# Weights' words and stores on ScalarE's queue, early words, unread products and a fifth weight buffer in an attention and Fourier-mixing kernel

## Chip, cores and metric

One core of one Trainium2 chip. The metric is the device time of one execution in microseconds (us). Each version was run several times; every run quoted here is fast (the program is on one core, and no run lay over 1.5% above the fastest of its kernel).

## The reference, cut to what matters

```python
B, H, S, Dh = 8, 8, 576, 64          # batches, heads, tokens, head width; D = 512
q_s = softmax(q, over Dh);  k_s = softmax(k, over S)
x   = q_s @ (k_s^T v)                # per batch and head, then heads side by side: (B, S, 512)
u   = x + real(fft2(x))              # over tokens and channels of a batch
un  = layer_norm(u)
out = u + relu(un @ w1) @ w2         # w1: 512 x 2048, w2: 2048 x 512
```

## The kernel before

The eight batches and one shared group of left-over tokens go through "rounds". A round has an **up phase** (un @ w1, relu) and a **down phase** (@ w2), each as seven half-size products (Strassen's scheme in Winograd's form). The attention, transform and normalising of the *next* batch are merged into these two phases as side steps. After the start TensorE has hardly a pause.

The weights arrive as 64-bit words. In the **start** they are converted once on the chip: 16 pairs of tiles (8 for w1, 8 for w2), each 2 halves of 128 x 512. A pair is converted, combined (four sums and differences) and stored to scratch memory (w1s, w2s), from which each round loads it again. What follows is cut.

```python
def wtile(self):                                   # ring of weight tiles, for words, pairs and reloads
    return self.work.tile([P, NP, HD], F32, tag="w", name="w", bufs=4)

def convert(self, place, t):                       # one half
    ...                                            # hi, lo: the two 32-bit halves of each word
    nc.scalar.activation(lo, lo.bitcast(U32), ACT.Copy, scale=2.0 ** -29)
    V.tensor_scalar(out=ti, in0=hi, ... shift left 3, and mask)
    V.scalar_tensor_tensor(out=ti, in0=hi, ... sign and top exponent bits | ti)
    nc.scalar.activation(hi, hi, ACT.Abs)
    V.scalar_tensor_tensor(out=t, in0=hi, scalar=least, in1=t, op0=is_ge, op1=mult)
    nc.gpsimd.tensor_tensor(out=ti, in0=ti, in1=lo, op=ALU.add)      # "the adder"

def prepare(self, layer, p, places):               # one pair
    w = self.wtile()
    for i in range(2): self.convert(places[i], ...)
    (b_side if layer else a_side)(..., nc.gpsimd, nc.vector)         # four combinations, split
    nc.sync.dma_start(w1s or w2s, w[:, 0:7, :])                      # SyncE issues the store

# per round g:
cut = len(side) * 2 // 3                           # two thirds of the next batch's steps in the up phase
merged(first (g == 0: with the weights) or up steps, side[:cut])
merged(down, side[cut:] + norm(g + 1))
```

## Time and profile before

| | before |
|---|---|
| median of 3 runs (range) | 1390.59 us (1386.94 to 1391.18) |
| span in the trace | 1384.5 us |
| first up-product / first down-product | 110.2 / 289.8 us |
| from the first down-product to the end | 1094.7 us |

The two times in the third row are the starts of the first matmul of the up line and of the down line in TensorE's timeline. They split the span into "start" and "rest". The lines of the profile are in the prediction.

### The profile page before, as it was taken

Reading aid. Unit: us, or ns where it says so; the run is one execution under the profiler, and the core shown is the slowest. Engines: PE = TensorE matmul, PEld = TensorE weight load, DVE = VectorE, ACT = ScalarE, POOL = GpSimd, SP = SyncE. Lnnn points to the kernel's source line nnn. Section 1 sums busy time; section 2 is a strip of 40 time slices with the busy share of each in tenths; the row PEclk is TensorE's granted clock in tenths of the full one; section 3 lists DMA queues with packets and bytes.
Section 4 is the critical chain, followed back from the end, with each engine's and each line's share of the span. In section 5 each row is a group of like instructions: output and inputs, shape, how many; then the busy total and the mean of one; then the engine's idle time right before and its main releaser. Section 6 shows DMA issues by size and latency. Waiting matters only on the chain.

```text
span 1384.5 us, 14661 instructions
## 1 busy us (share of the span) xinstructions
PE 1226.2 (89%) x5676; PEld 1003.1 (72%) x5676; DVE 580.0 (42%) x1146; ACT 326.7 (24%) x590; POOL 422.1 (30%) x350
## 2 busy tenths in 40 slices
PE   4578677399899998999999999999999999999992
PEld 3437563288787876788778877887788778788882
DVE  3948876821513254335713542364234242502200
ACT  2624342410310142114301421142014101201200
POOL 1624566710530125003600450045013401321310
PEclk7558785589999999999999999999999999999996
DMA  5922334575342543156424542454253335455421
GB/s 170 306 68 69 137 128 163 190 265 164 141 152 88 172 159 146 67 167 198 158 98 138 193 159 77 145 197 152 88 146 130 150 103 174 150 178 179 165 102 45
DMA packets 90279, 203.46 MB, mean 147 GB/s; under 512 B 22241, under 2 KB 56033, under 8 KB 82145
## 3 DMA queue, kind: packets, MB, share of 16 engines
q1 hardware_dynamic: 90208, 202.52, 43.2%
q8 instruction: 45, 0.74, 0.2%
q14 instruction: 26, 0.20, 0.0%
HBM read 177.33 MB, written 29.88 MB: 150 GB/s over the span
## 4 chain that ended last, share of the span: by engine, by line
PE 74%; DVE 10%; POOL 6%; DMA 4%; issue 2%; ACT 1%; SPq 0%; POOLq 0%; DVEq 0%; ACTq 0%
PE bb L590 14%; PE bb L555 11%; PE bc L590 9%; PE ba L590 9%; PE ba L555 7%; PE bc L555 6%; PE acc L402 5%; DMA q<-in_q_dram 3%; PE acc L289 3%; PE acc L427 2%; POOL w L192 1%; PE acc L424 1%; PE tr L486 1%; PE acc L405 1%; POOL eo L384 1%
## 5 line engine op out<-in xcount | busy, mean ns | idle before, releaser
L555 PE MATMUL bb<-unT,w 128*128 128x256 f32 x864 | 218.8, 395 | 46.6 <-DVE u L525 39.6
L555 PEld LDWEIGHTS bb<-unT,w 128*128 128x128 f32 x864 | 166.5, 197 | 78.3 <-DVE u L525 46.3
L590 PE MATMUL bb<-w,h 128*128 128x256 f32 x864 | 198.5, 381 | 0.0
L590 PEld LDWEIGHTS bb<-w,h 128*128 128x128 f32 x864 | 161.5, 190 | 28.4 <-issue 7.3
L555 PE MATMUL ba<-unT,w 128*128 128x256 f32 x576 | 142.5, 387 | 0.0
L196 POOL TENSOR_TENSOR h<-h 128x512 f32<-128x512 f32 x36 | 46.1, 1279 | 313.4 <-ACT h L567 313.4
L555 PE MATMUL bc<-unT,w 128*128 128x256 f32 x576 | 140.5, 381 | 0.0
L590 PE MATMUL bc<-w,h 128*128 128x256 f32 x576 | 131.4, 381 | 0.0
L590 PE MATMUL ba<-w,h 128*128 128x256 f32 x576 | 128.0, 379 | 0.0
L590 PEld LDWEIGHTS bc<-w,h 128*128 128x128 f32 x576 | 107.5, 190 | 18.0 <-issue 4.4
L555 PEld LDWEIGHTS ba<-unT,w 128*128 128x128 f32 x576 | 109.2, 194 | 15.7 <-issue 1.0
L590 PEld LDWEIGHTS ba<-w,h 128*128 128x128 f32 x576 | 109.2, 190 | 15.4 <-issue 0.8
L555 PEld LDWEIGHTS bc<-unT,w 128*128 128x128 f32 x576 | 107.0, 190 | 15.3 <-DVE h L566 0.9
L567 ACT ACTIVATE h<-h 128x512 f32<-128x512 f32 x108 | 68.1, 631 | 190.8 <-DVE h L566 190.5
L604 POOL TENSOR_TENSOR x<-x,u 128x512 f32<-128x512 f32 x18 | 23.3, 1293 | 254.4 <-DVE u L528 172.2
L402 PE MATMUL acc<-ft,eo 128*128 128x289 f32 (+3 forms) x240 | 83.3, 472 | 7.5 <-POOL eo L386 7.4
L402 PEld LDWEIGHTS acc<-ft,eo 128*128 128x128 f32 (+3 forms) x240 | 39.6, 183 | 42.3 <-issue 26.0
L525 DVE TENSOR_TENSOR u<-bb,s 128x512 f32<-128x512 f32 x45 | 31.0, 689 | 89.1 <-PE bb L555 54.3
L318 POOL TENSOR_TENSOR q<-q,qm 128x512 f32<-128x512 f32 x36 | 41.8, 1170 | 82.2 <-DVE qm L317 33.1
L528 DVE TENSOR_TENSOR u<-bb,s 128x512 f32<-128x512 f32 x45 | 31.0, 689 | 77.5 <-PE bb L555 45.4
L289 PE MATMUL acc<-v,ks 128*128 128x128 f32 (+1 forms) x320 | 55.5, 317 | 6.1 <-ACT ks L277 4.1
L566 DVE TENSOR_TENSOR h<-bc,u 128x512 f32<-128x512 f32 x72 | 49.6, 689 | 24.0 <-PE bc L555 23.0
(134 smaller groups left out, 1540.0 us busy)
## 6 DMA issues: line engine op xcount, KB each, us to landing
w<-w2s SPq DMA_DIRECT2D x63, 1024.0 KB
w<-w1s SPq DMA_DIRECT2D x64, 896.0 KB
k<-in_kT_dram SPq DMA_DIRECT2D x32, 288.0 KB
h<-in_w_dram SPq DMA_DIRECT2D x18, 512.0 KB
v<-in_v_dram SPq DMA_DIRECT2D x32, 256.0 KB
q<-in_q_dram SPq DMA_DIRECT2D x32, 256.0 KB
w1s<-w SPq DMA_DIRECT2D x8, 896.0 KB
w2s<-w SPq DMA_DIRECT2D x8, 896.0 KB
```

The source lines that it names most:

```text
L196: e1.tensor_tensor(out=at(4), in0=at(2), in1=at(3), op=ALU.add)
L289: nc.tensor.matmul(pk, lhsT=ks[0:n, c, :], rhs=v[0:n, c, :], start=(c == 0), stop=(c == NC - 1))
L318: nc.gpsimd.tensor_tensor(out=heads, in0=heads, in1=spread(m), op=ALU.subtract)
L402: nc.tensor.matmul(pz, lhsT=eo[c][int(odds)][s, cols], rhs=self.ft[s, 3 * int(odds) + c, :], start=(c == 0), stop=(c == 2 and odds))
L427: nc.tensor.matmul(pb, lhsT=z(2 + k), rhs=self.cd[:, 2 + k, 0:HD - 1], start=(k == 0), stop=(k == 1))
L525: V.tensor_tensor(out=temp("u2"), in0=box["bb"][:], in1=box["s1"][:], op=ALU.add)
L528: V.tensor_tensor(out=temp("u3"), in0=box["bb"][:], in1=box["s1"][:], op=ALU.add)
L555: nc.tensor.matmul(bank()[:, i, :], lhsT=w[:, A_AT[m], k * P:(k + 1) * P], rhs=unT[:, B_AT[m], k, :], start=first and i == 0 and k == 0, s ...
L566: V.tensor_tensor(out=at(i), in0=bank[:], in1=u[:], op=ALU.add)
L567: nc.scalar.activation(at(i), at(i), ACT.Relu)
L590: nc.tensor.matmul(bank()[:, i, :], lhsT=h[:, p, A_AT[m], i * P:(i + 1) * P], rhs=w[:, p, :], start=first and i == 0 and p == 0, stop=p == ...
L604: nc.gpsimd.tensor_tensor(out=x, in0=x, in1=t[:], op=ALU.add)
```

## The change

Its intent: shorten the start, in which TensorE idles, by preparing the weights earlier and with less work on GpSimd. ScalarE's queue issues the words' loads and the stores of combinations, so that they don't stand among SyncE's loads; words of seven pairs are fetched during the first attention; the conversion loses one two-input instruction; all combinations go to VectorE; the first batch's queries have six buffers in place of three; 30 unread products keep the array busy; and only one third of the second batch's steps is merged into the first up phase. Smaller parts are that a tail's first query rows come in one transfer, and that each pair's store is issued one pair later. One line deepens the ring of weight tiles from four to five.

```diff
-        return self.work.tile([P, NP, HD], F32, tag="w", name="w", bufs=4)
+        return self.work.tile([P, NP, HD], F32, tag="w", name="w", bufs=5)
 ... words():  self.nc.sync.dma_start  ->  self.nc.scalar.dma_start
 ... convert(place, t, adder):
+        nc.scalar.activation(t, hi.bitcast(F32), ACT.Abs)
+        V.tensor_scalar_max(t, t, least)
+        V.tensor_scalar(out=ti, in0=ti, ... shift left 3, and mask)
         V.scalar_tensor_tensor(out=ti, in0=hi, ... | ti)
+        nc.scalar.activation(lo, lo.bitcast(U32), ACT.Copy, scale=2.0 ** -29)
+        adder.tensor_tensor(out=ti, in0=ti, in1=lo, op=ALU.add)          # adder: GpSimd, as before
-        (...)(lambda i: w[:, i, :], nc.gpsimd, nc.vector)
+        (...)(lambda i: w[:, i, :], self.nc.vector, self.nc.vector)
+    def send(self, layer, p, w):                   # called one pair later
+        self.nc.scalar.dma_start(to, w[:, 0:7, :])
+    def warm(self, t, n):                          # n unread products of 128 x 128 x 256
+    def follow(self, t):                           # after a key's or query's exponential:
+        if self.first:                             # touch the place (gate), then fetch early words
+            self.nc.scalar.copy(place[0:1, 0:1], t[0:1, 0:1]); run()
-        q = self.work.tile([P, D], F32, tag="q", name="q", bufs=3)
+        q = self.halves()[:, 0:D]                  # first batch: ring of six
-        cut = len(side) * 2 // 3
+        cut = len(side) * (1 if g == 0 else 2) // 3
```

## The prediction

> **What bounds the kernel now.** I read the engine totals first, then busy time by stretch, then waits and groups inside the first stretch, then the queue that issues the transfers. The totals say TensorE, but an average over stages can hide a stage with another limit. So I cut the span where the programme changes: attention of the first batch (to 62 us), its transform and normalising (to 110), the first batch's up-products (to 204), the rest of the weights' preparation (to 290), and everything after.
>
> ```profile
> PE 1226.2 (89%) x5676; PEld 1003.1 (72%) x5676; DVE 580.0 (42%) x1146; ACT 326.7 (24%) x590; POOL 422.1 (30%) x350
> ...
> PEclk7558785589999999999999999999999999999996
> ```
>
> ```profile
> core 0: us, PE busy (x) PEld busy (x) DVE busy (x) ACT busy (x) POOL busy (x), PEclk, DMA share, GB/s
> 0.00:62.00 62.00, 27.33 (x114) 21.32 (x115) 37.81 (x79) 24.44 (x44) 22.76 (x30) 0.66 0.75 240
> 62.00:110.00 48.00, 34.59 (x91) 18.86 (x90) 28.31 (x65) 16.47 (x31) 16.25 (x15) 0.57 0.31 100
> 110.00:204.00 94.00, 70.14 (x341) 59.99 (x340) 77.31 (x126) 34.23 (x63) 52.27 (x43) 0.86 0.32 108
> 204.00:290.00 86.00, 52.81 (x161) 33.83 (x160) 59.30 (x113) 29.97 (x53) 50.61 (x42) 0.54 0.62 204
> 290.00:1384.50 1094.50, 1041.38 (x4977) 869.05 (x4975) 377.24 (x765) 221.60 (x401) 280.21 (x221) 0.98 0.42 143
> ```
>
> The last row is 95% TensorE at a granted clock of 0.98: the change can win almost nothing there. The first 290 us hold 185 us of TensorE, partly at half clock. There VectorE is busiest (203 us of 290, 77 of 94 while the first up-products run). Everything to be won is in these 290 us. The waits there say why TensorE stands:
>
> ```profile
> PE tr L486 <- DVE eo L479: 34.0, 3, 23.3
> PE bb L555 <- DVE u L525: 23.9, 3, 8.7
> ```
>
> The first are transposes waiting for normalised rows, the longest (23.3 us) while VectorE works off weights. The second are up-products whose PSUM bank VectorE empties late because weights stand ahead of it in its queue. The weights' own groups:
>
> ```profile
> L192 POOL TENSOR_TENSOR w<-w,h 128x512 int32<-128x512 int32 x18 | 25.9, 1444 | 26.9 <-DVE w L191 23.7 <-DVE qrec L322 2.5 <-issue 0.7
> L191 DVE SCALAR_TENSOR_TENSOR w<-h,w 128x512 f32<-128x512 f32 x18 | 22.1, 1232 | 1.2 <-ACT h L190 1.1
> L187 DVE SCALAR_TENSOR_TENSOR w<-h,w 128x512 int32<-128x512 int32 x18 | 16.4, 914 | 0.0
> ```
>
> VectorE is almost never idle before its two (1.2 and 0.0 us), and both run above their undisturbed 0.69 us (seen at 83.6 and 85.1 us, where GpSimd is still). The end of the stage is one chain: the last combination is stored, lands, is loaded again, and only then may the down-products start:
>
> ```profile
> 275.77 0.38 SPq L219 DMA_DIRECT2D w2s<-w  x1
> ...
> 280.52 2.12 SPq L230 DMA_DIRECT2D w<-w2s  x4
> ```
>
> The first down-product starts at 289.8 us: 14 us after that store was issued.
>
> **What the Trainium skill says.** "SBUF — State Buffer", section "Who interferes with whom": a VectorE instruction with two SBUF inputs, or in a 2-port mode, excludes a GpSimd instruction that reads SBUF, and one blocks the other wholly. The trace agrees: L191 has a mean of 1.23 us against 0.69 undisturbed. "VectorE: DVE Perf Modes", section "Mode 2×_2P": one-source fp32 instructions get two elements a cycle, two-source ones don't. The trace agrees: a one-source instruction on 512 columns (L185) takes 0.42 us, a two-source one 0.69. "DMA: Bandwidth & Descriptors", section "Issuing engines are not separate DMA queues": issuing from another engine saves only the sequencer's time. I take from this that ScalarE issuing brings no bandwidth, but frees transfers from the waits of SyncE's queue. "TensorE: Matmul & The Clock Gate", section "HAM oscillation": idle gaps over some 3.4 us return the array to half clock. The trace agrees in direction: after a 3.5 us gap at 68.5 us the transform's products run at about 0.57 us each, against 0.28 at 206 us.
>
> **The change, part by part.**
> (1) Conversion: per half tile of 128x512, 0.42 + 0.69 + 0.69 = 1.80 us on VectorE become 0.42 + 0.42 + 0.69 = 1.53, as a maximum with a constant replaces a two-source comparison. 32 halves save 8.6 us.
> (2) Combinations: all four per pair go to VectorE. Before, GpSimd had two of four in layer 1 and three of four in layer 2. Undisturbed, 256 columns cost VectorE 0.40 us: 8 x 2 + 8 x 3 = 40 instructions add 16 us to VectorE and take 40 x 0.87 = 35 us from GpSimd (L196, L197, L203, L205 and L206 have means of 0.82 to 0.89). So VectorE's own demand grows by 16 - 8.6 = 7.4 us. In return the alternation VectorE, GpSimd, VectorE, GpSimd per pair is gone, and less GpSimd work blocks VectorE: in the start VectorE was busy 203 us for some 172 us of undisturbed durations, so blocking was about 30 us; GpSimd's 142 us there fall by 35, a quarter, so about 8 us of it go. The two sums cancel. The gain must come from order.
> (3) Order. The changed kernel's instruction order, as built, shows the first words' loads at the head of ScalarE's queue (before: issued at 25.4 us), stores no longer between SyncE's loads (SyncE waited 62.9 us for them at L216 and 42.4 at L219), and the second batch's queries, fold, transform and normalising behind the last weights on VectorE, most of the products of these inside the first down-products on TensorE. That takes from the start about 35 us of VectorE work (queries 4 x 2.4, folds and copies 6, mix 5, normalising and combining 9, keys of the third batch 6).
> (4) The unread products. The description announces 36; the build has 30 (four key tiles, two tail and four query tiles, three each), or 60 in the trace. At 0.43 us warm, 0.86 cold, that is 13 to 26 us beside attention's waits; TensorE is busy 27 of the first 62 us. If they keep the array warm through the transform, its 18 + 10 products take about 13 us instead of 28.
>
> Now the new start, from summed durations along VectorE's order. To the first combining of the normalised tile it holds 74 us (before 64, reached at 112 us). Attention itself no longer waits for query tiles (a six-deep ring instead of three) or for ten small loads: I put its end at 50 us instead of 62, and the start of the up-products at 98 instead of 110, VectorE-bound, since stalls and blocking fill the 24 us above the sum. Up-products: 48 us of TensorE (224 products of 0.216 x 2), 8 us of keys of which I count 4 as hidden in stalls, and bank waits: after the first and third group VectorE converts two pairs (2 x 4.7 us plus keys) ahead of the emptying of the next, while TensorE can go on for 5.2 us (12 products): 6 + 8 us. That makes 66 us, to 164 (before: 94). Two of layer 2's pairs are then done. The other six: two buffers, each bound for a load of about 6.5 us (1 MB) and 6 us of conversion, so 6.3 us a pair where it was about 11 (stores issued at 226.5, 237.2, 248.1): 164 + 5 for the first load + 38 = 207. Then the 14 us of store and load, tied with the last queries, which need about as long: the down-products start at 221 instead of 290, **69 us earlier**.
>
> Given back: TensorE work that was done before 290 and now stands in its saturated part: half the transform 4.4 us, mix 4.3, normalising transposes 2, keys and queries of the third batch about 10: 21 us. I add 2 us of new stalls in the first down-products for the chain that moved there. Net 69 - 21 - 2 = 46 us. 1390.6 - 46 = **1345 us**.
>
> **The rivals.**
> A. The ScalarE queue becomes the bound. Its engine is in order: a store that waits for VectorE, or a load that waits for a free buffer, holds the activations behind it. For: nine loads in a row took SyncE 10.97 us to issue at 41.1 us, and 40 issues now stand among conversions and PSUM copies. Against: ScalarE is busy only 105 of 290 us. This would eat 20 to 25 us: about 1368.
> B. VectorE's demand is all that counts: 7 us more, and the moved 35 us come back as stalls in the down-products. For: it is the busiest engine there. Against: after 290 it is busy 377 of 1094 us, so moved work has room. This makes 1385 to 1395.
> C. The array stays warm through the transform and attention shrinks more than I think: another 10 to 15 us, about 1332. Against: the gap before the transform's tail remains, since the fold's third piece comes from GpSimd behind two weight additions, and VectorE holds 47 us of work between attention and up-products anyway.
> D. The early words slow the first keys: at the head three loads of 512 KB stand ungated. That is 1.5 MB, at 240 GB/s (the first row's rate) 6 us; partly hidden, a few us.
>
> **Range and chances.** The 69 us are the weak term: 15 us either way on up-products and pairs, A or C on top. Net gain 20 to 72 us gives 1318 to 1370. The 2% line is at 1362.8, a net gain of 28 us, which needs the start to shrink by 51 of my 69. I give faster 0.82, same 0.16, slower 0.02.
>
> **What would show it.** Right: first down-product between 205 and 237 us; six layer 2 pairs 6 to 7.5 us apart; bank waits of the up-products below 24 us; TensorE's wait for normalised rows (34 us) below 15; after the start, TensorE still above 93% busy. Wrong: a first down-product after 245 us with ScalarE waiting for buffers or combinations (A); a start near 220 with new TensorE waits of over 20 us in the first down-products (B). The unread products' step is right if clock in the first 50 us is above 0.66 and the transform still runs at about 0.57 us a product; C if it runs at 0.28.

## The result, and the profile after

The changed kernel takes **1428.61 us** (median of 4 runs, 1427.71 to 1428.9) against 1390.68 (4 runs, 1386.94 to 1391.18). The ratio is 1.0278, 95% interval 1.0259 to 1.0296: 2.8% slower. (Ratios here are the mean time of one kernel's fast runs over that of the other's fast runs of the same rounds, so not quite the ratio of the medians.)

The first up-product comes at 117.3 us (before: 110.2) and the first down-product at 274.6 (289.8): the start is 15.2 us shorter. The rest is 1152.5 us (1094.7): **57.8 us longer**. The page and the stretches of the changed kernel:

```profile
PE 1237.2 (87%) x5736; PEld 1015.8 (71%) x5736; DVE 577.2 (40%) x1186; ACT 323.9 (23%) x597; POOL 380.6 (27%) x310
...
PEclk8868875799999999999999999999999999999996
```

```profile
core 0: us, PE busy (x) PEld busy (x) DVE busy (x) ACT busy (x) POOL busy (x), PEclk, DMA share, GB/s
0.00:62.00 62.00, 37.27 (x172) 30.13 (x173) 29.52 (x72) 19.06 (x42) 15.35 (x24) 0.83 0.80 253
62.00:110.00 48.00, 26.97 (x78) 14.69 (x76) 37.10 (x83) 19.92 (x39) 18.98 (x16) 0.69 0.21 84
110.00:204.00 94.00, 70.77 (x300) 58.00 (x301) 65.15 (x114) 28.18 (x51) 34.48 (x25) 0.83 0.30 104
204.00:290.00 86.00, 34.73 (x149) 27.81 (x148) 50.39 (x98) 23.24 (x43) 31.35 (x26) 0.64 0.64 226
290.00:1384.50 1094.50, 1050.63 (x4967) 870.68 (x4966) 393.00 (x818) 233.52 (x424) 280.46 (x221) 0.97 0.40 140
```

Against the same table in the prediction: in the first 290 us GpSimd fell from 142 to 100 us, VectorE from 203 to 182. The granted clock of the first stretch rose from 0.66 to 0.83. Yet TensorE did less there, 170 us against 185, though the unread products (13 to 26 us by the prediction's estimate) are in the 170. The fourth row stands out: 34.73 us of TensorE in 86 where it had been 52.81. What is not done there must be done later.

**Later rounds.** The waits of TensorE after 290 us, first of the kernel before, then of the changed one (columns: who waits for whom, us in all, times, longest):

```profile
PE bb L555 <- DVE u L525: 15.7, 6, 3.3
PE bb L555 <- DVE u L528: 7.0, 4, 4.1
```

```profile
PE tr L296 <- ACT k L271: 21.7, 6, 3.6
PE bb L585 <- DVE u L555: 12.7, 4, 3.8
```

A kind of wait has come up that was not there: the key transposes (L296) of the next batch wait for the key's exponential (L271), six times 3.6 us, about once a round. One of them in TensorE's timeline (start, duration, what, count; in brackets the idle time before it):

```profile
509.10 1.89 PE L585 MATMUL bc<-unT,w 128*128 128x256 f32 x8
514.61 1.11 PE L296 MATMUL tr<-ident,k 128*128 128x128 f32 x4 [3.62 <-ACT k L271]
...
516.59 2.67 PE L311 MATMUL acc<-v,ks 128*128 128x128 f32 x10
...
524.26 1.47 PE L311 MATMUL acc<-v,ks 128*128 128x128 f32 x10
```

After the 3.62 us of idleness the same ten products take 2.67 us, and 1.47 some 8 us later: each wait also costs some us at half clock (the granted clock is 1.00 from 505 to 510 us and 0.50 from 514.6 to 519.2). In the groups by shape this shows as a longer mean of the products that come next, first before, then after:

```profile
L555 PE MATMUL ba<-unT,w 128*128 128x256 f32 x576 | 142.5, 387 | 0.0
```

```profile
L585 PE MATMUL ba<-unT,w 128*128 128x256 f32 x576 | 150.9, 402 | 0.9 <-ACT s L552 0.8
```

VectorE's timeline of the same moment says why the exponential is late: its key's maximum (L268) stands in VectorE's queue behind three emptyings of up-products (L596), the last two of which wait for TensorE.

```profile
506.57 0.69 DVE L596 TENSOR_TENSOR h<-bc,u 128x512 f32<-128x512 f32 x1
509.30 0.69 DVE L596 TENSOR_TENSOR h<-bb,s 128x512 f32<-128x512 f32 x1 [2.04 <-PE bb L585]
511.03 0.69 DVE L596 TENSOR_TENSOR h<-bc,u 128x512 f32<-128x512 f32 x1 [1.03 <-PE bc L585]
511.64 0.74 DVE L268 TENSOR_REDUCE km<-k 128x1 f32<-128x576 f32 x1
```

Almost nothing in the change's code touches the later rounds except the ring of weight tiles, which serves the reloads there (the second tail's queries also come in three transfers fewer). The instruction orders of both kernels, as built, showed more: the kernel before *with five buffers* and the changed kernel have their last 2426 TensorE instructions and 292 ScalarE instructions in the same order; the changed kernel *with four buffers* shares its last 2405 and 296 with the kernel before. Four other parts undone in builds with five buffers (unread products, ScalarE's issuing, the combinations, the one third) left that order as it was. No run has five buffers in the old order, so the ring and the order that comes with it are not parted.

**The start.** Waits of TensorE from 62 to 204 us:

```profile
PE tr L516 <- DVE eo L509: 11.9, 1, 11.9
PE bb L585 <- DVE u L555: 9.2, 2, 8.3
```

The second, the up-products' wait for a bank, was 23.9 us before and is shorter. The first looks shorter too (34.0 before), but is not: of the 34.0 us only 9.7 were the first batch's, against 11.9 now. The other 24.4 were waits for the second batch's rows, whose transposes now come after the first down-product (from 328.85 us). And ScalarE now stands. In the first 40 us it stands until earlier words have landed (first fence, here ahead of a copy of keys), from 200 us on for words and for VectorE's last combination, whose store is next in its queue, with the next pair's Abs (L187) behind it (second fence), and another 6.0 us for GpSimd's adder:

```profile
ACT ks L297 <- DMA h<-in_w_dram: 7.4, 1, 7.4
```

```profile
ACT w L187 <- DMA w<-in_w_dram: 11.7, 1, 11.7
ACT w L187 <- DVE w L209: 10.9, 2, 5.4
```

And TensorE, from 204 to 290 us, stands for the second batch's queries, whose copy out of PSUM (L366) is in that same queue:

```profile
PE acc L378 <- ACT qT L366: 33.2, 2, 32.5
```

The stores of the second layer's pairs, which the prediction wanted 6.3 us apart, are (43.25 / 5 =) 8.65 us apart in the last five intervals, after a gap of 21. With this gap, the last six intervals have a mean of 10.7 us, no shorter than the 10.5 of the kernel before:

```profile
216.15 0.37 ACTq L225 DMA_DIRECT2D w2s<-w  x1
...
259.40 0.37 ACTq L225 DMA_DIRECT2D w2s<-w  x1
```

### The profile page after: what moved, and what is told of

Its sections match the earlier page's. It is cut to its first block, busy times and chain, and to the rows that moved or that the text cites. A ratio compares the mean times of both kernels' runs of the same rounds, so it can differ in the third digit from the quotient of the medians.

```text
span 1427.1 us, 14777 instructions
## 1 busy us (share of the span) xinstructions
PE 1237.2 (87%) x5736; PEld 1015.8 (71%) x5736; DVE 577.2 (40%) x1186; ACT 323.9 (23%) x597; POOL 380.6 (27%) x310
## 4 chain that ended last, share of the span: by engine, by line
PE 68%; DVE 6%; POOL 4%; ACT 2%; issue 1%; DMA 1%; ACTq 0%; POOLq 0%; DVEq 0%; SPq 0%
PE bb L620 13%; PE bb L585 10%; PE ba L620 9%; PE bc L620 9%; PE bc L585 6%; PE ba L585 6%; PE acc L432 4%; PE acc L311 3%; PE acc L457 1%; POOL q L345 1%; PE tr L296 1%; PE tr L516 1%; PE acc L454 1%; PE acc L378 1%; POOL eo L414 1%
## 5 line engine op out<-in xcount | busy, mean ns | idle before, releaser
L585 PEld LDWEIGHTS bb<-unT,w 128*128 128x128 f32 x864 | 170.1, 200 | 65.0 <-DVE u L555 24.6
L585 PE MATMUL ba<-unT,w 128*128 128x256 f32 x576 | 150.9, 402 | 0.9 <-ACT s L552 0.8
L585 PEld LDWEIGHTS ba<-unT,w 128*128 128x128 f32 x576 | 113.7, 203 | 18.9 <-issue 1.9
L620 PEld LDWEIGHTS ba<-w,h 128*128 128x128 f32 x576 | 110.2, 192 | 16.9 <-issue 2.0
L432 PE MATMUL acc<-ft,eo 128*128 128x289 f32 (+3 forms) x240 | 78.0, 448 | 11.2 <-POOL eo L416 8.0
L378 PE MATMUL acc<-kvr,qT 128*128 128x128 f32 x256 | 37.4, 295 | 43.9 <-ACT qT L366 33.2
L378 PEld LDWEIGHTS acc<-kvr,qT 128*128 128x128 f32 x256 | 34.2, 205 | 48.3 <-ACT qT L366 34.7
L311 PE MATMUL acc<-v,ks 128*128 128x128 f32 (+1 forms) x320 | 57.7, 326 | 11.9 <-DVE ks L300 7.7
```

The lines of the kernel that those rows point to most:

```text
L311: nc.tensor.matmul(pk, lhsT=ks[0:n, c, :], rhs=v[0:n, c, :], start=(c == 0), stop=(c == NC - 1))
L378: nc.tensor.matmul(px[:, r * P:(r + 1) * P], lhsT=qT[:, r, :], rhs=self.kvr[b % 2][:, r, :], start=True, stop=True)
L432: nc.tensor.matmul(pz, lhsT=eo[c][int(odds)][s, cols], rhs=self.ft[s, 3 * int(odds) + c, :], start=(c == 0), stop=(c == 2 and odds))
L585: nc.tensor.matmul(bank()[:, i, :], lhsT=w[:, A_AT[m], k * P:(k + 1) * P], rhs=unT[:, B_AT[m], k, :], start=first and i == 0 and k == 0, s ...
L620: nc.tensor.matmul(bank()[:, i, :], lhsT=h[:, p, A_AT[m], i * P:(i + 1) * P], rhs=w[:, p, :], start=first and i == 0 and p == 0, stop=p == ...
```

## The experiments

**Theory.** (a) The fifth buffer makes the scheduler choose another order for every round, which costs some 25 us. (b) The stores in ScalarE's in-order queue hold back work of the second batch. **Rivals**: the later rounds are longer because work moved into them; early words delay the first keys; the array's clock; the pairs are paced by something that the change leaves alone.

Times are medians; "rest" is from the first down-product to the end of the profiled run. The kernel before was run beside each group and lay between 1387.5 and 1389.0.

| run | time | ratio to before (95%) | first up / first down | rest |
|---|---|---|---|---|
| before | 1389.0 | | 110.2 / 289.8 | 1094.7 |
| changed | 1428.6 | 1.0278 (1.0259, 1.0296) | 117.3 / 274.6 | 1152.5 |
| e1 changed, four buffers | 1406.3 | 1.0108 (1.0076, 1.0140) | 113.4 / 279.1 | 1117.7 |
| e2 before, five buffers | 1407.1 | 1.0128 (1.0107, 1.0150) | 109.5 / 278.5 | 1124.5 |
| e3 e1, no unread products | 1401.4 | 1.0083 (1.0061, 1.0106) | 110.0 / 276.9 | 1122.3 |
| e4 e1, stores on SyncE | 1388.1 | 0.9989 (0.9970, 1.0007) | 109.5 / 276.8 | 1108.2 |
| e5 e4, late words | 1396.0 | 1.0063 (1.0038, 1.0088) | 115.9 / 284.6 | 1109.3 |
| e6 e4, words on SyncE | 1385.2 | 0.9985 (0.9956, 1.0013) | 112.5 / 273.6 | 1108.5 |
| e7 e4, combinations split | 1390.2 | 1.0018 (0.9988, 1.0047) | 111.2 / 273.6 | 1113.0 |
| e8 before, conversion and combinations | 1383.2 | 0.9962 (0.9934, 0.9991) | 103.2 / 272.1 | 1108.4 |
| e9 e8, ring of six | 1377.7 | 0.9917 (0.9902, 0.9933) | 99.9 / 268.2 | 1108.4 |
| e10 e9, unread products | 1378.3 | 0.9925 (0.9906, 0.9944) | 101.8 / 270.8 | 1110.3 |
| e11 e8, adder on VectorE (or) | 1362.0 | 0.9810 (0.9792, 0.9828) | 101.2 / 251.4 | 1107.0 |
| e12 e10, adder on VectorE | 1357.2 | 0.9782 (0.9760, 0.9804) | 95.8 / 244.8 | 1108.2 |
| e13 e4, adder on VectorE | 1375.2 | 0.9897 (0.9876, 0.9918) | 106.9 / 265.1 | 1106.9 |
| e14 e6, adder on VectorE | 1369.9 | 0.9862 (0.9830, 0.9893) | 113.5 / 244.7 | 1121.2 |
| e15 e11, add in place of or | 1363.7 | 0.9807 (0.9762, 0.9851) | 101.5 / 252.3 | 1110.2 |
| **e16 e12, no unread products** | **1355.0** | **0.9754 (0.9730, 0.9777)** | 93.7 / 244.6 | 1108.0 |
| e17 e14, two thirds | 1369.0 | 0.9863 (0.9834, 0.9892) | 112.1 / 256.6 | 1111.4 |
| e18 e16, five buffers | 1374.9 | 0.9899 (0.9883, 0.9916) | 93.8 / 236.7 | 1136.5 |

All results were correct. Two cautions. Every edit lets the scheduler reorder the start, so a difference of some 3 us between two versions need not be the edit's own. And the starts and rests are of one profiled run each, which may lie off the median: e1's is 7.7 us below it, e10's 4.6 above it, that of the kernel before 2.8 below it. The order of the later rounds is the same in all versions with four buffers, which I checked in the builds.

### e1 and e2: the fifth buffer

```diff
 e1, changed kernel:   bufs=5  ->  bufs=4
 e2, kernel before:    bufs=4  ->  bufs=5
```

> The changed kernel with the ring of weight tiles put back from five buffers to four, all else as changed. Theory (the fifth buffer lets the scheduler put the second job's evacuations ahead of the third key tile's maximum and exponential in every later round, and TensorE then stands up to 3.6 us and drops to half clock for some us each round): the waits of the key transposes on the exponential after 290 us (21.7 us in six) disappear and the time falls by about 25 us, to 1400. Rival (the later rounds are longer because work moved out of the start into them): the later rounds stay as they are, 1425 to 1430.

> The kernel before with five weight buffers in place of four and nothing else. Theory (fifth buffer): the same six or so waits of the key transposes appear after 290 us and the time rises by about 25 us, to 1415. Rival (moved work makes the later rounds longer): 1388 to 1393, as before.

Measured: 1406.3 and 1407.1. The theory holds both ways: 22 us come off the changed kernel, 18 are put on the kernel before. (e1's four runs spread from 1398.6 to 1407.4; its profiled run is the fastest.) In e1 the wait of the transposes after 290 us is gone, and the first wait is one that the kernel before has, too; in e2 the new wait is there:

```profile
PE bb L585 <- DVE u L555: 18.5, 6, 4.1
```

```profile
PE tr L276 <- ACT k L265: 18.1, 5, 3.6
```

The table shows something that the times hide. The fifth buffer *shortens* the start, by 4.5 us (279.1 to 274.6) and 11.3 us (289.8 to 278.5), as it was surely meant to. It lengthens the rest by 34.8 and 29.8. TensorE's timeline says where: against e1, the second and the fourth to seventh up phases of the changed kernel are 6.3 to 8.6 us longer each (the fifth takes 79.6 us, 71.6 in e1), while every down phase after the first lasts the same to 0.1 us.

### e3, e10, e12 and e16: the unread products

```diff
-        if it[1] == 0:
-            self.warm(k, 3)          # and the same for q
```

> The changed kernel with four buffers and without the unread products. If these products hold the clock in the start as the prediction had it, the run is 5 us or more slower than the same with them (about 1405 if that is 1400). If the start is set by transfers and by the other engines' chain, and not by the array's clock, it is within 5 us of it, either way.

> As e9_ring with the unread products added, 30 of 128 by 128 by 256. Theory of the prediction (they hold the clock in the attention and in the transform behind it): 3 to 6 us faster than e9_ring. Theory since the run without them on the changed kernel with four buffers (1401 against 1406): 0 to 5 us slower than e9_ring, as the array is granted full speed for the wait and not for work on the path, and the products themselves take about 40 us of array time in the attention.

> Ring, unread products and the VectorE adder together on the kernel before with new conversion and combinations. If the gains of e9 and e11 add, and the unread products cost nothing: 1368 to 1376. If the start's gain is given back whichever way it is won: 1378 to 1384.

> As e12_all (1357.2) without the unread products. If they are worth nothing here too: 1355 to 1360. If they hold the clock for the transform, as the prediction had it: 1361 to 1366.

Measured: without them 1401.4 against 1406.3 (e3, e1), 1377.7 against 1378.3 (e9, e10), 1355.0 against 1357.2 (e16, e12). Three pairs, on three different bases, and each time they are worth nothing, or cost up to a few us; the intervals of each pair overlap. (The "40 us of array time" in the text of e10 is too much: in the first 62 us TensorE was busy 42.3 us with them and 33.8 without.) They do make the array faster there: the first products of the queries take 0.13 us each in e10, and 0.26 in e9. But the attention does not end earlier: the first transform product comes at 64.9 us with them and 65.8 without (e1, e3), at 53.2 and 52.0 (e10, e9), at 52.3 and 52.5 (e12, e16). The granted clock of the first 62 us is no sign of them: it rises from 0.70 (e3) to 0.83 (e1), but falls from 0.97 (e9) to 0.84 (e10) and from 0.98 (e16) to 0.88 (e12). e12 came out better than its first theory.

### e4: stores back on SyncE

```diff
-        self.nc.scalar.dma_start(to, w[:, 0:7, :])
+        self.nc.sync.dma_start(to, w[:, 0:7, :])
```

> The changed kernel with four buffers and the stores of the combinations issued by SyncE again, the words still by ScalarE. Theory (ScalarE's in-order queue stands at each store until the last combination is ready, with the next pair's work behind it): the second layer's pairs come at 6 to 7 us in place of 8.7 and the run is about 10 us faster than the same with stores on ScalarE (1390 if that is 1400). Rival (the pairs are bound by VectorE and GpSimd sharing, whoever issues): pairs still at 8 to 9 us, no difference over 3 us.

Measured: 1388.1, 18 us less than e1 by the medians (12 us by the profiled runs), more than I expected, and **not by the way I expected**: the second layer's pairs are no closer (the last seven stores lie 9.3 us apart), and the first down-product comes only 2.3 us earlier. What changed is how much of the second batch TensorE gets done meanwhile. The stretch from 204 to 290 us, e1 and then e4:

```profile
204.00:290.00 86.00, 34.86 (x140) 27.97 (x139) 52.52 (x104) 24.95 (x46) 31.99 (x26) 0.62 0.63 216
```

```profile
204.00:290.00 86.00, 51.91 (x171) 34.75 (x170) 55.66 (x109) 23.35 (x45) 29.07 (x23) 0.62 0.56 197
```

17 us more of TensorE (51.91 - 34.86) in the same time, because ScalarE copies the second batch's queries out of PSUM earlier. In e1 TensorE waits 33.0 us for the second copy, which starts at 245.9 us; in e4 the first two copies are through at 219.9, and the longest such wait is 14.9 us. The first down phase shrinks from 61.9 to 51.8 us. Two things changed at once here. No store stands in ScalarE's queue any more (10.9 us of waiting for the last combination in e1), and with the stores gone the scheduler put the second copy behind three pairs' conversions where e1 has five (counted in ScalarE's order as built, from the same copy of keys). ScalarE still stands: from 200 to 262 us it waits 33.5 us for words, adder and combinations in e1, and 24.4 for words and adder in e4. How much of the gain is the standing and how much the order, these runs do not part. Either way the queue cost by what stood behind it, not by the pace of the chain that it stood for.

### e5 and e6: when and by whom the words are issued

```diff
 e5:  follow(k) left out; follow(q) called twice; the second half of a place gated as well
 e6:  dma = self.nc.scalar.dma_start  ->  dma = self.nc.sync.dma_start
```

> As the run with four buffers and the stores on SyncE (1388), and besides the early words held back until the keys are through: both halves of a fetch wait for a query tile's exponential, two fetches a query, and no fetch waits for a key tile. Theory (the early words fill the DMA engines in the first 20 us and delay the keys, and this is why the attention does not end at 50): the fourth key maximum comes near 19 us as in the kernel before and not at 32, attention ends at 52 to 56 in place of 64, and the run takes 1376 to 1383. Rival (the start is bound behind the attention by conversions, the fold and the transform, so that earlier keys gain nothing, or later words take it back): 1385 to 1391.

> As the run with four buffers and the stores on SyncE (1388), with the words issued by SyncE as well, so that ScalarE issues nothing. Theory (ScalarE's in-order queue holds its own computing back while it waits to issue words: 7.4 and 3.8 us in the first 40 us, 11.7 us before one pair): 3 to 8 us faster, 1380 to 1385. Rival (SyncE then stands at a gated fetch with the loads of keys, queries and values behind it): 1390 to 1400.

Measured: e5 1396.0, 8 us slower than e4, a miss of both theories; e6 1385.2, at the edge of what its theory said, but its interval overlaps with e4's. In e5 the fourth key's maximum comes at 21.4 us as the theory had it (33.0 in e4), so the early words do delay the keys. But now the words stand in the queries' way: ScalarE waits 7.9 us for words to land while it should copy queries (first fence), and the first up-product comes 6 us later. In e6 the keys are early as well (20.8 us) and the queries late (the last maximum at 59 us, 45.6 in e4), as SyncE issues gated words before them; TensorE waits for the queries (second fence; 19.2 of the 41.1 us are the first batch's, the rest the second's):

```profile
ACT qT L370 <- DMA h<-in_w_dram: 7.9, 1, 7.9
```

```profile
PE tr L360 <- DVE q L352: 41.1, 3, 21.8
```

Wherever the early words are put, something of the attention waits for them: in all three versions the first up-product comes at 109 to 116 us.

### e7 and e8: conversion and combinations

```diff
 e7, from e4:      combinations (vector, vector)  ->  (gpsimd, vector)
 e8, from before:  the new convert(), adder on GpSimd; combinations (gpsimd, vector) -> (vector, vector)
```

> As the run with four buffers and the stores on SyncE (1388), with the seven combinations split between GpSimd and VectorE again as in the kernel before. Theory of the prediction (these operations cost 35 us on GpSimd and 16 us on VectorE, and on GpSimd they are on the chain of a pair): about 10 us slower, 1395 to 1402. Rival (pairs are paced by the adders on GpSimd, which share with VectorE in both cases): within 3 us of 1388.

> The kernel before with nothing but the new conversion (five operations, the adders on GpSimd as before) and all combinations on VectorE: its words and stores stay on SyncE, its order of steps, its four buffers, no unread products. Theory (these two parts are the sound part of the change; together they take 35 us off GpSimd and put some 8 on VectorE in the start, and the pairs after 200 us come closer): 8 to 15 us faster than before, 1374 to 1381. Rival (the start is bound by something the arithmetic does not touch): 1386 to 1391.

Measured: e7 1390.2, 2 us from e4, with overlapping intervals: who makes the combinations hardly matters. e8 1383.2, 0.4% faster than before, short of the 8 to 15 us: the start is 17.7 us shorter, and 13.7 of them come back in the rest, 10.9 in the second up phase (71.3 us, 60.4 before), where a part of the third batch's keys now stands (5 of 20 transposes, 20 of 40 products with v); the kernel before has them all in the start.

### e9: the ring of six

```diff
 from e8:  q = work.tile(..., bufs=3)  ->  q = self.halves()[:, 0:D]  (first batch); first rows of the tail in one transfer
```

> The kernel before with the new conversion and all combinations on VectorE (measured 1383.2) plus one more part of the change: the first batch's query tiles in the six-buffer ring and their first rows loaded in one transfer; words and stores on SyncE, four weight buffers, no unread products. Theory (with the words behind them in the queue, the earlier queries shorten the attention, which ended at 65 us in the kernel before): queries' maxima all by 36 us in place of 47, up-products start 5 to 8 us earlier than 103 us, run 1375 to 1380. Rival (what the queries win the words lose, as in the run with late words): 1381 to 1386.

Measured: 1377.7, some 6 us less than e8. First up-product 99.9 us (103.2). The up-products start 3.3 us earlier, less than the 5 to 8 expected, but the time is in the theory's range.

### e11 and e15: the adder

```diff
 e11, from e8:  nc.gpsimd.tensor_tensor(out=ti, in0=ti, in1=lo, op=ALU.add)  ->  V.tensor_tensor(..., op=ALU.bitwise_or)
 e15, from e8:  the same                                                     ->  V.tensor_tensor(..., op=ALU.add)
```

> The kernel before with the new conversion and all combinations on VectorE (measured 1383.2), and the adder of each half on VectorE, as a bitwise or in place of an integer add (the last bits of a word may differ, well inside the tolerance), so that GpSimd has no part in a pair. Theory (the pairs are paced by the GpSimd adder: VectorE waits for it and its single-input operations take 1.4 us beside it in place of 0.41): pairs of the second layer at 6 to 7 us, first down-product 8 to 15 us earlier than 272 us; of this a half or more is given back in the next two phases, since the second batch's work then falls there: run 1376 to 1381. Rival (paced by transfers of words): no pair closer, 1382 to 1386.

> As e11_vector_adder (1362.0), with an integer add on VectorE in place of the or; the order of all instructions is the same. If it is the engine that matters, 1359 to 1366; if the or itself was cheaper, up to 1372. The result may be slightly off in the last bits.

Measured: 1362.0 and 1363.7, against 1383.2 of e8: 21 and 20 us, where the theory of e11 had said 2 to 7. It is the largest single gain, from an operation that the change leaves on GpSimd. The order of all instructions of the two is the same, and so is the time: it is the engine that matters. The Trainium skill, "GPSIMD Engine Reference", section "Engine selection", says that an add of 32-bit integers is exact on GpSimd while the ordinary elementwise path computes in fp32, which is presumably why the adder was there. The results of both VectorE forms were within the tolerance; no run here measured by how much the last bits differ. An adder on GpSimd took 1.41 us (e8: 26.0 + 11.0 + 8.1 us for 32, from the groups of the first 290 us); on VectorE 0.68 to 0.92. The stores of the second layer's pairs lie 7.6 us apart in e11 (mean of the last six intervals, of which the last takes 11), in e8 9.1. Moving the adder takes away two things, the turns between the engines and the slowing of VectorE's instructions beside GpSimd (in e8 two of the masks at L187 take 1.39 us in place of 0.42). These runs do not part them.

### e13, e14 and e17: the adder in the changed kernel itself

```diff
 e13, e14:  adder.tensor_tensor(..., op=ALU.add)  ->  V.tensor_tensor(..., op=ALU.bitwise_or), on e4 and on e6
 e17, from e14:  cut = len(side) * (1 if g == 0 else 2) // 3  ->  len(side) * 2 // 3
```

> The changed kernel with four buffers and stores on SyncE (1388.1), and the adder on VectorE as an or. Theory (the term that failed is the pair's pace, set by the GpSimd adder): pairs at 6 to 7 us, first down-product 15 to 25 us earlier than 277 us, run 1360 to 1370. Rival (the early words and the order of steps themselves hold it, whatever the adder): 1380 to 1388.

> As e13 with the words on SyncE as well (1385.2 with the GpSimd adder). Theory: 1358 to 1368, within 5 us of e13. Rival: 1378 to 1386.

> As e14 (1369.9), with two thirds of the second batch's steps merged into the first up phase, as in the kernel before, in place of one third. Theory (one third leaves about 10 us of TensorE work to the down phase while TensorE idles in the start): first down phase 50 to 53 us in place of 63.0, run 1356 to 1364. Rival (more of that work ahead of the last pairs delays them by as much): 1367 to 1372.

Measured: 1375.2 and 1369.9. e13 falls between its two theories: its first down-product comes 11.7 us earlier, not 15 to 25, and its pairs are 8.2 us apart (last six intervals; 9.3 in e4), not 6 to 7. e14 is 2 us above its theory's range, with the first down-product 28.9 us earlier than e6's. Only its stores show the pace that the prediction had put into its sum:

```profile
191.00 0.38 SPq L225 DMA_DIRECT2D w2s<-w  x1
...
228.13 0.37 SPq L225 DMA_DIRECT2D w2s<-w  x1
```

Six intervals in 37.1 us: 6.2 us a pair (8.6 in e6; 7.8 in e17, with the same adder and queue).

e14 and e16 have their first down-product at the same time (244.7 and 244.6), yet e14 takes 15 us more. e17 tested one cause and it failed: with two thirds merged, the first down phase is as short as foreseen (52.0 in place of 63.0), but the first down-product comes 12 us later; the sum is the same. What remains between e17 and e16 is a start that is 18.4 us behind at the first up-product (112.1 against 93.7). Both have the VectorE adder, the ring of six, and SyncE issuing. The early words between the first keys and queries are the plainest difference and agree with e5 and e6, but the order of the steps, the store's delay by one pair and the unread products differ as well, and I didn't part these.

### e18: the fifth buffer on the best version

```diff
-        return self.work.tile([P, NP, HD], F32, tag="w", name="w", bufs=4)
+        return self.work.tile([P, NP, HD], F32, tag="w", name="w", bufs=5)
```

> As e16 (1355.0) with five weight buffers. Theory (the order that five buffers give in every round costs the same whatever the start): 15 to 23 us slower, 1370 to 1378, with key transposes waiting for the exponential after 290 us. Rival (the cost belongs to the start of the kernels it was measured on): within 5 us, 1351 to 1360.

Measured: 1374.9, 20 us more than e16: the cost does not depend on the start. It shortens that by 7.9 us and lengthens the rest by 28.5, with the same wait:

```profile
PE tr L276 <- ACT k L265: 21.8, 6, 3.6
```

**Best version**: e16, the kernel before with the new conversion, all combinations and the adder on VectorE, and the ring of six, 1355.0 us: 2.5% faster than before and about 5% faster than the changed kernel (0.9754 / 1.0278).

## Why the prediction was wrong, point by point

It said 1345 with a range to 1370 and 0.02 for slower; it is 1428.6. Its sum was "69 us earlier, 23 given back". Measured: 15.2 earlier, 57.8 given back. So it failed twice: in the start, 54 us short, and in the rest, where a term of 27 to 35 us was missing.

- **"What bounds the kernel now"**: right that all is to be won in the first 290 us, and that TensorE stands there behind VectorE. Wrong in that it looked no further. "After the start TensorE still above 93% busy" came true (1050.63 of 1094.5 us, 96%) and was no proof: of the 35 us that the fifth buffer costs after the start (changed against e1), 18 are waits (43.7 us of them after 290 us, against 26.0 in e1), and some 9 are slower products, which count as busy (the group shown above: 150.9 us, 141.9 in e1). The rest of the 35 I have not assigned.
- **The missing term: the fifth buffer.** It stands in the diff, and the prediction doesn't mention it. The order as built was at hand and I read it for the start alone. Net worth +22 us (e1), +18 (e2), +20 (e18). The scheduler's reason for the other order is open; that the order comes with the buffer is shown by the builds, and what the two cost together by the runs.
- **The start, "69 us earlier".** The sum had the first up-product at 98 us, the last at 164, the last pair's store at 207 and the first down-product at 221. They came at 117.3, 200.6, 259.4 and 274.6. So 19 of the missing 54 us were lost before the up-products, 17 in them, 16 in the remaining pairs and 1 in the final store and load. The up-products' waits for a bank, 14 us in the sum, were right (9.2 + 2.9 + 2.8 us); but TensorE had 63.9 us of work there, with 11 us of keys and some products at half clock, in place of the 52 counted. The waits for normalised rows were misread: of the 34.0 us that the prediction shows, 24.4, with the longest, fall after 204 us and are the second batch's.
- **(1) Conversion, 8.6 us off VectorE, and (2) combinations, 35 us off GpSimd**: happened (GpSimd's busy time in the start fell by 42 us; VectorE's by 21, which includes work that was only moved behind the start), and gained little: 5 us together (e8), 2 us, within the noise, for the combinations alone (e7). "The two sums cancel. The gain must come from order" was right in its first half.
- **(3) "I put its end at 50 us"**: it ended at 64, as before (first transform product at 64.4 us, 65.4 before). Rival D ("a few us") was too small: the fourth key's maximum came at 32.4 us in place of 18.7. The DMA share in the first 20 us is 0.96 where it had been 0.66; I had reckoned with the mean rate of the stretch, 240 GB/s, as if it had been free.
- **(3) "6.3 us a pair"**: measured 8.65, after a gap of 21. I took 6 us of conversion and a load of 6.5 us as the bounds and left out the adder on GpSimd, though the prediction showed its line (1.44 us each, and idle before it mostly for VectorE: the two take turns). With the adder on VectorE the first down-product comes 12 to 29 us earlier (e13, e11, e14) and the pace is 8.2, 7.6 and 6.2 us. So the adder is part of this term; the words on ScalarE's queue (e13 against e14) go with another part, and the gap of 21 us was not tested by itself.
- **Rival A** named ScalarE's queue, at 20 to 25 us, and the prediction gave its test: "a first down-product after 245 us with ScalarE waiting for buffers or combinations". This happened, and costs 18 us (e4), but through the queries that stand behind the stores and the order that comes with them: the words on ScalarE cost 3 us, within the noise, while the adder is on GpSimd (e6 against e4).
- **(4) Unread products**: "right if clock in the first 50 us is above 0.66 and the transform still runs at about 0.57 us a product". The clock of the first 50 us was 0.80, and the transform's products took 0.48 and 0.55 us. But the sign could not decide: the same 50 us have 0.70 in the kernel before, and 1.00 in e8 and e9, which have no unread products. The sum gave them no term of its own, and the runs agree: they are worth nothing (e3, e10, e16).
- **Given back**: 23 us predicted. In the twelve edited versions with four buffers, SyncE's stores and a first down phase of at most 53 us (all of these but e7 and e14) the rest is 1107 to 1111 us, so 12 to 17 us are given back however much the start wins, most of it in the second up phase (68 to 71 us in e4, e8, e11 and e16, 60.4 before). There the third batch's keys now stand (20 of 20 transposes in e4, e11 and e16, none before), as the sum's item "keys and queries of the third batch about 10" had it. The changed kernel's 57.8 are about 13 of this kind, 10 from the stores on ScalarE (1117.7 against 1108.2), and 35 from the fifth buffer (1152.5 against 1117.7). The last two shares rest on e1's profiled run, 7.7 us faster than its median: if its usual run loses those 7.7 us in the rest, they are about 18 and 27 (an estimate).

Still open: which part of the early words' scheme makes e17's start 14 us slower in the end than e16's.

## What to carry to other kernels

A deeper ring is not free even where memory is: compare the order of *every* stage as built, with and without it, because a scheduler that sees one more free buffer may reorder stages that you didn't mean to touch. Put a transfer that has to wait into the queue of an engine whose next work can wait as well; look at what stands behind it, not at what it serves. And before taking work off an engine because it is busy, find the operation on which the other engine waits: moving 35 us of combinations from GpSimd gained 2 us, moving 45 us of adders gained 20.

## What the Trainium skill lacked or had wrong

- "DMA: Bandwidth & Descriptors", section "Issuing engines are not separate DMA queues", speaks of what issuing on several engines saves. It lacks the cost on an engine that computes: sixteen stores on ScalarE, with the order that came with them, cost 18 us (e4 against e1); in e1 ScalarE stood 10.9 us for the last combinations, and TensorE 33.0 us for a copy queued behind.
- No page covers the effect of a ring's depth on the order of other stages: five weight buffers in place of four shorten the start by 5 to 11 us and lengthen the rest by 29 to 35 (e1, e2, e18).
